# A state-space scan with a three-way maxout FFN: the first block in another order, and weight decoding in portions

## The chip, the cores and the metric

The kernel runs on one core of a Trainium2 chip. The metric is the device time of one execution in microseconds (us). TensorE (PE) has two clock levels, 1.2 and 2.4 GHz; a granted clock of 1.00 in a row is the higher one. PEld is PE's weight load, DVE is VectorE, ACT ScalarE, POOL GpSimd, SP SyncE, which issues DMAs.

## The reference, cut to what matters

```
log_a = log(clip(a, 1e-6, 1))                   # a: (4 batches, 8 heads, 768 steps)
for each chunk:
    cum = cumsum(log_a[chunk])
    L[i,j] = exp(cum[i] - cum[j]) for i >= j, else 0
    y = ((C @ B.T) * L) @ x + (C @ state) * exp(cum)
    state = exp(cum[-1]) * state + sum_j exp(cum[-1] - cum[j]) * B[j] x[j]
X = y as (3072 tokens, 256)
h = max(X @ w1, X @ w2, X @ w3)                 # w: 256 x 768
out = h @ w_out                                 # w_out: 768 x 256
```

x is (4, 8, 768, 32), B and C are (4, 8, 768, 16), all float32. The four weights are float64 in DRAM.

## The kernel before, in words

The 768 steps are cut into NC = 6 blocks of 128 steps; a block holds 4 batches x 8 heads. For a block, B and C are transposed on PE (trB, trC) and copied by ACT to BT and, once for even and once for odd heads, to CT. `scan_scores` makes the products of B and C for two batches in four PSUM banks, and DVE multiplies them into L (L406), which holds the decays exp(cum_i - cum_j). `scan_out` multiplies by x (and, from block 1 on, adds the carried state, L419) and copies y to yT. `scan_state` carries the state on.

The FFN of a block has six up groups, `up(c, f)`, and two down groups, `down(c, u)`. An up group makes three products of yT with w1, w2 and w3, each in one of three PSUM banks of the tag "ffn": ACT copies the first to m (L449), DVE takes the maximum with the second and with the third (L451). A product is four matmul instructions in the trace. A down group multiplies h with w_out, ACT copies the result to ob, and SP stores it.

The order of each engine's work is the order in which the program issues it (a manual schedule). Between the groups of block c, the pieces of the scan of block c + 1 are issued by hand, at group number k.

Decays of block 0 come from `spread_first` (PE spreads cum over the partitions, four banks for two batches; there are five banks of the tag "att"). For batches 0 and 1, POOL fills `below` and DVE adds (L293), then ACT takes exp (L295). For batches 2 and 3, PE adds a mask by a product with the identity (L265) and ACT takes exp with ncum as bias, one head at a time (L301). From block 1 on, cum is stored in DRAM (`cums`), `decay_load` spreads it to all partitions in four DMAs of 512 KB, and a `decay_part` is one POOL select for a batch (L323) and four exps on ACT for half of its heads (L327). `last_load` brings E in eight small DMAs.

A weight is fetched in 12 jobs of 512 KB (nine of w1 to w3, three of w_out) by SP into `rb`. `decode` turns a job to float32: Abs on ACT (L162), a clip (L163) and a shift (L166) on DVE, a scaled copy on ACT (L170), an add on POOL (L171), and the sign step on DVE (L172), which waits for the add. Jobs 0 to 2 serve the first two up groups, 3 to 5 the next two, 6 to 8 the last two, 9 to 11 the down groups. Three jobs are decoded ahead of the FFN, the others after each group of block 0.

SP's queue before: a, B, C, six small loads of the rest of a (a_sb, L110), two jobs, x, one job, cums, three jobs, B and C of block 1, one job, L, x and E of block 1, and then the jobs that are left.

Of the kernel before, what the change touches and what calls it, by code (L numbers as in the profile page):

```python
# [18 lines left out]
def kernel(  # L19
# [24 lines left out]
    P = 128  # L44
# [21 lines left out]
    wraw = ctx.enter_context(tc.tile_pool(name="wraw", bufs=7))  # L66
    wtmp = ctx.enter_context(tc.tile_pool(name="wtmp", bufs=2))
# [39 lines left out]
    a_sb = const.tile([R, 2, P], FP32, name="a_sb")  # L107
    for c in range(NC):
        w, k = divmod(c, NC // 2)
        nc.sync.dma_start(  # L110
            out=a_sb[k * BH:(k + 1) * BH, w], in_=a_rows[:, c * P:(c + 1) * P])


# [33 lines left out]
    def decode():  # L147

        if not fetched:
            return  # L150
# [4 lines left out]
        def temp(name):  # L155
            return wtmp.tile(shape, U32, tag=name, name=name)

        u = temp("w_u")
        nc.scalar.activation(u.bitcast(FP32), hi.bitcast(FP32), AF.Abs)  # L162
        nc.vector.tensor_scalar(  # L163
            out=u.bitcast(FP32), in0=u.bitcast(FP32), scalar1=SMALL, scalar2=LARGE,
            op0=ALU.max, op1=ALU.min)
        nc.vector.tensor_scalar(  # L166
            out=u, in0=u, scalar1=3, scalar2=None, op0=ALU.logical_shift_left)

        r = temp("w_r")
        nc.scalar.activation(r.bitcast(FP32), lo, AF.Copy, bias=2.0, scale=2.0 ** -51)  # L170
        nc.gpsimd.tensor_tensor(out=r, in0=u, in1=r, op=ALU.add)  # L171
        nc.vector.scalar_tensor_tensor(  # L172
            out=dst.bitcast(U32), in0=hi.rearrange("p (k f) -> p k f", k=2), scalar=0x80000000,
            in1=r.rearrange("p (k f) -> p k f", k=2), op0=ALU.bitwise_and, op1=ALU.bitwise_or)

    fetch()
    fetch()
    load(0, "x")
# [22 lines left out]
    mask = const.tile([P, HALF, P], FP32, name="mask")  # L201
    nc.gpsimd.memset(mask, 0.0)
    nc.gpsimd.affine_select(
        out=mask, in_=mask, pattern=[[0, HALF], [1, P]], compare_op=ALU.is_ge, fill=MASKED,
# [5 lines left out]
    def running(rows, src, name):  # L210

        nc.vector.tensor_scalar(
            out=src, in0=src, scalar1=1e-6, scalar2=1.0, op0=ALU.max, op1=ALU.min)
        lg = const.tile(list(src.shape), FP32, name=name + "_lg")
        nc.scalar.activation(lg, src, AF.Ln)
        for w in range(src.shape[1]):
            nc.vector.tensor_tensor_scan(
                out=src[:, w], data0=keep[0:rows], data1=lg[:, w], initial=0.0,
                op0=ALU.mult, op1=ALU.add)
        return src  # L220
# [23 lines left out]
    cum0 = running(P, a0.unsqueeze(1), "first")  # L244
    t = by_token(BH, cum0, "ncum0", -1.0)
    ncum[0] = t[:, 0]
# [13 lines left out]
    def spread_first(b0, masked):  # L260
        for i in range(2):
            for g in range(2):
                spread[b0 + i, g] = bank = att_bank([P, HALF, P], "spread")
                if masked:
                    nc.tensor.matmul(  # L265
                        out=bank.rearrange("p k i -> p (k i)"), lhsT=ident,
                        rhs=mask.rearrange("p k i -> p (k i)"), start=True, stop=False,
                        skip_group_check=True)
        for k in range(HALF):
            for i in range(2):  # L270
                for g in range(2):
                    rows = slice((2 * i + g) * BH, (2 * i + g + 1) * BH)
                    n = (b0 + i) * NH + g * HALF + k
                    nc.tensor.matmul(
                        out=spread[b0 + i, g][:, k],
                        lhsT=pick[rows, n:n + 1].to_broadcast([BH, P]), rhs=cum0[rows, 0],
                        start=(k == 0 and not masked), stop=True,
                        tile_position=((2 * i + g) * BH, 0),
                        skip_group_check=True)

    def below(b):

        t = att.tile([P, NH, P], FP32, tag="below", name="below")
        nc.gpsimd.affine_select(
            out=t, in_=ncum[0][:, b * NH:(b + 1) * NH].unsqueeze(2).to_broadcast([P, NH, P]),
            pattern=[[0, NH], [1, P]], compare_op=ALU.is_ge, fill=MASKED, base=0,
            channel_multiplier=-1)
        return t

    def first_by_sum(b, t):  # L290
        for g in range(2):
            part = L0[:, b, g * HALF:(g + 1) * HALF]
            nc.vector.tensor_tensor(  # L293
                out=part, in0=spread[b, g], in1=t[:, g * HALF:(g + 1) * HALF], op=ALU.add)
            nc.scalar.activation(part, part, AF.Exp)  # L295

    def first_by_bias(b):
        for g in range(2):
            for k in range(HALF):
                h = g * HALF + k  # L300
                nc.scalar.activation(  # L301
                    L0[:, b, h], spread[b, g][:, k], AF.Exp,
                    bias=ncum[0][:, b * NH + h:b * NH + h + 1], scale=1.0)
# [34 lines left out]
    def scan_in(c, bank):  # L338
        st = blocks[c]
        if c < NC - 1:  # L340
            st["Bd"] = Bd = att.tile([P, BH, N], FP32, tag="Bd", name="Bd")
            nc.gpsimd.tensor_tensor(
                out=Bd, in0=st["B"], in1=from_j[c].unsqueeze(2).to_broadcast([P, BH, N]),
                op=ALU.mult)
        tr = {}
        for name in ("B", "C"):
            tr[name] = bank([HN, NB, P], "tr" + name)
            for b in range(NB):
                nc.tensor.transpose(  # L349
                    out=tr[name][:, b],  # L350
                    in_=st[name][:, b * NH:(b + 1) * NH].rearrange("s h n -> s (h n)"),
                    identity=ident)
        st["BT"] = BT = att.tile([HN, NB, P], FP32, tag="BT", name="BT")
        nc.scalar.copy(out=BT, in_=tr["B"])  # L354

        st["CT"] = CT = att.tile([HN, NB, 2, P], FP32, tag="CT", name="CT")
        for g in range(2):
            nc.scalar.mul(CT[:, :, g], tr["C"], parity[:, g:g + 1])
        if c > 0:
# [3 lines left out]
            nc.vector.tensor_tensor(out=Cd, in0=tr["C"], in1=E, op=ALU.mult)  # L363

    def scan_state(c):
        if c == NC - 1:
            return
# [24 lines left out]
    def scan_scores(c, b0):  # L392
        st = blocks[c]
        L = Ls[c]
        banks = [att_bank([P, 2, 2, P], "s") for _ in range(NP)]
        for i in range(2):
            b = b0 + i
            for r in range(NP):
# [4 lines left out]
                    start=(i == 0), stop=True, tile_position=(r * PN, 0), skip_group_check=True)  # L403
        for r in range(NP):
            M = L[:, b0:b0 + 2, 2 * r:2 * r + 2]
            nc.vector.tensor_tensor(out=M, in0=banks[r], in1=M, op=ALU.mult)  # L406

    def scan_out(c):
# [3 lines left out]
        ys = [att_bank([P, NB, P], "y") for _ in range(KD)]  # L412
# [22 lines left out]
    hT = {}  # L435

    def up(c, f):
# [3 lines left out]
        for i in range(3):  # L441
# [27 lines left out]
    spread_first(0, False)  # L469
    from_j[0] = by_token(BH, fj0, "from_j0", 1.0)[:, 0]  # L470
    sums = [below(b) for b in range(2)]
    for b in range(2):
        first_by_sum(b, sums[b])
    scan_in(0, ffn_bank)
    spread_first(2, True)
    cum = running(R, a_sb, "all")
    nc.sync.dma_start(
        out=cums.rearrange("c k s -> (c k) s").rearrange("(w r) s -> r w s", w=2), in_=cum)
    scan_scores(0, 0)
    for b in range(2, NB):  # L480
        first_by_bias(b)
    scan_scores(0, 2)
    fj = from_last(R, cum, "fj")
    ncums = by_token(R, cum, "ncums", -1.0)
    from_js = by_token(R, fj, "from_js", 1.0)
    for c in range(1, NC):
        ncum[c], from_j[c] = ncums[:, c], from_js[:, c]
    for _ in range(3):
        fetch()
    load(1, "B")  # L490
    load(1, "C")
    scan_out(0)
    for _ in range(3):
        decode()
    scan_state(0)
    fetch()
    decay_load(1)
    load(1, "x")
    last_load(1)

    pieces = [(up, f) for f in range(NF)] + [(down, u) for u in range(NB // 2)]
    parts = decay_parts(1)
    for c in range(NC):
        n = c + 1
        for k, (g, i) in enumerate(pieces):
            g(c, i)
            for _ in range(2 - k % 2):
                decode()  # L510
                if weight_jobs:
                    fetch()
            if n < NC:
                if k == 1:
                    scan_in(n, att_bank)
                if k == 3:
                    scan_scores(n, 0)
                if k == 4:
                    scan_state(n)
                if k == 5:  # L520
                    scan_scores(n, 2)
                if k == 6:
                    scan_out(n)
            if n + 1 < NC:
                if k == 4:
                    decay_load(n + 1)
                    load(n + 1, "B")
                    load(n + 1, "C")
                    load(n + 1, "x")
                    last_load(n + 1)  # L530
                    parts += decay_parts(n + 1)
            if k > 0 or c > 0:
                for _ in range(2):
                    if parts:
                        decay_part(*parts.pop(0))
# [30 lines left out]
```

## Time and profile before

| what | value |
|---|---|
| median of 3 runs (range) | 347.91 us (347.3 to 348.58) |
| profiled execution, its own time | 347.55 us |
| its span, first to last instruction | 345.7 us |
| granted PE clock, mean | 0.951 |
| busy share: PE, DVE, ACT, POOL | 92%, 32%, 34%, 15% |

The page gives busy time by engine; the share is a mean over stages. Chains and waits say what ended last in a stage; windows give busy time, granted clock and traffic in a stretch. The execution's own time is 1.85 us more than the span, which the instructions do not cover.

### The profile page before, as it was taken

How to read it: one execution, taken by the hardware profiler on the slowest of the kernel's cores; microseconds unless marked ns; L12 is line 12 of the kernel's file. 1: busy time of each engine (PE TensorE's matmuls, PEld its weight loads, DVE VectorE, ACT ScalarE, POOL GpSimd, SP SyncE). 2: the span in 40 equal slices, each digit the busy share in tenths (PEclk: the TensorE clock that was granted, in tenths of full speed). 3: DMA queues.
4: the chain of work that ended last, by engine and by line, in shares of the span. 5: the costliest groups of instructions: out<-in, count | busy, mean ns of one | idle time of the engine just before them, and what ended most of it. 6: DMA issues, size and time to landing. Idle time of an engine off the chain costs nothing.

```text
span 345.7 us, 4497 instructions
## 1 busy us (share of the span) xinstructions
PE 316.5 (92%) x1742; PEld 180.7 (52%) x1742; DVE 110.8 (32%) x182; ACT 117.1 (34%) x293; POOL 51.8 (15%) x58
## 2 busy tenths in 40 slices
PE   4895978595699999999999999999999999999995
PEld 3464333242486444684444874445854447744474
DVE  3162554573600334401342303354012443022310
ACT  3625445461537400544314272206443010111001
POOL 6002233235520002400006000005000000000000
PEclk9956998879589999999999999999999999999999
DMA  7999889800003960007910019900000000100001
GB/s 74 199 274 255 163 317 279 112 2 0 1 32 101 236 88 2 1 32 254 139 34 1 32 58 247 117 5 2 32 31 0 0 0 2 41 22 0 0 0 61
DMA packets 87333, 28.06 MB, mean 81 GB/s; under 512 B 75537, under 2 KB 81681, under 8 KB 87313
## 3 DMA queue, kind: packets, MB, share of 16 engines
q1 hardware_dynamic: 87216, 27.76, 35.6%
q8 instruction: 13, 0.21, 0.3%
q14 instruction: 8, 0.06, 0.1%
q10 hardware_dynamic: 96, 0.03, 0.0%
HBM read 24.54 MB, written 3.24 MB: 80 GB/s over the span
## 4 chain that ended last, share of the span: by engine, by line
PE 79%; ACT 5%; POOL 5%; DVE 5%; DMA 2%; issue 2%; SPq 0%; POOLq 0%; DVEq 0%; ACTq 0%
PE up L444 48%; PE o L459 19%; PE s L400 4%; PE y L427 4%; POOL w_r L171 3%; ACT L L327 3%; DMA raw_C<-in_C_dram 2%; PE y L419 1%; POOL L L323 1%; PE spread L265 1%; DVE w_u L166 1%; PE trC L349 1%; DVE w_u L163 1%; ACT L L301 1%; DVE w L172 1%
## 5 line engine op out<-in xcount | busy, mean ns | idle before, releaser
L444 PE MATMUL up<-yT,w 128*128 128x512 f32 x432 | 196.4, 610 | 11.8 <-DVE w L172 7.3
L444 PEld LDWEIGHTS up<-yT,w 128*128 128x128 f32 x432 | 82.7, 195 | 112.9 <-issue 92.4
L459 PE MATMUL o<-wo,h 128*128 128x256 f32 x288 | 68.8, 397 | 7.0 <-ACT m L449 5.5
L451 DVE TENSOR_TENSOR m<-m,up 128x512 f32<-128x512 f32 x36 | 24.7, 687 | 146.6 <-PE up L444 77.8
L459 PEld LDWEIGHTS o<-wo,h 128*128 128x128 f32 x288 | 56.1, 198 | 18.7 <-ACT m L449 5.9
L327 ACT ACTIVATE L<-L,ncums 128x128 f32<-128x128 f32 x160 | 48.9, 391 | 43.6 <-POOL L L323 43.6
L449 ACT COPY m<-up 128x512 f32<-128x512 f32 x36 | 20.9, 580 | 87.2 <-PE up L444 87.2
L451 DVE TENSOR_TENSOR h<-m,up 128x512 f32<-128x512 f32 x36 | 24.8, 688 | 27.8 <-PE up L444 27.0
L406 DVE TENSOR_TENSOR L<-s,L 128x512 f32<-128x512 f32 x48 | 29.8, 682 | 9.9 <-PE s L400 9.9
L463 ACT COPY ob<-o 128x512 f32<-128x512 f32 x12 | 7.0, 586 | 51.6 <-PE o L459 40.2
L171 POOL TENSOR_TENSOR w_r<-w_u,w_r 128x512 uint32<-128x512 uint32 x12 | 15.2, 1265 | 60.4 <-DVE w_u L166 55.0
L323 POOL TENSOR_SCALAR_AFFINE_SELECT L<-L 128x1024 f32<-128x1024 f32 x20 | 22.2, 1138 | 0.0
L400 PE MATMUL s<-CT,BT 32*128 32x256 f32 x192 | 18.7, 439 | 1.5 <-ACT L L301 1.5
L400 PEld LDWEIGHTS s<-CT,BT 32*128 32x128 f32 x192 | 11.7, 201 | 11.4 <-issue 7.6
L385 POOL TENSOR_TENSOR old<-S,E 128x256 f32<-128x256 f32 x4 | 2.5, 622 | 76.3 <-issue 76.3
L427 PE MATMUL y<-L,raw_x 128*32 128x128 f32 x384 | 13.4, 299 | 0.0
L172 DVE SCALAR_TENSOR_TENSOR w<-rb,w_r 128x512 uint32<-128x512 uint32 x9 | 8.8, 977 | 13.2 <-POOL w_r L171 13.2
L432 ACT COPY yT<-y 128x512 f32<-128x512 f32 x12 | 6.4, 589 | 18.5 <-PE y L427 18.5
L427 PEld LDWEIGHTS y<-L,raw_x 128*32 128x32 f32 x384 | 11.4, 120 | 1.3 <-issue 0.9
L388 POOL TENSOR_TENSOR S<-S,old 128x256 f32<-128x256 f32 x4 | 2.9, 726 | 47.0 <-DVE S L380 47.0
L162 ACT ACTIVATE w_u<-rb 128x512 f32<-128x512 f32 x12 | 8.1, 672 | 1.4 <-POOL w_r L171 1.4
L354 ACT COPY BT<-trB 128x512 f32<-128x512 f32 x6 | 3.5, 583 | 14.4 <-PE trB L349 14.4
(61 smaller groups left out, 110.2 us busy)
## 6 DMA issues: line engine op xcount, KB each, us to landing
L<-cums SPq DMA_DIRECT2D x20, 512.0 KB, 6.5
rb<-in_moe_w_dram SPq DMA_DIRECT2D x9, 512.0 KB, 5.0
raw_x<-in_x_dram SPq DMA_DIRECT2D x6, 512.0 KB, 7.8
out_dram<-ob SPq DMA_DIRECT2D x12, 256.0 KB, 2.2
raw_B<-in_B_dram SPq DMA_DIRECT2D x6, 256.0 KB, 9.1
raw_C<-in_C_dram SPq DMA_DIRECT2D x6, 256.0 KB, 11.0
rb<-in_moe_w_out_dram SPq DMA_DIRECT2D x3, 512.0 KB, 5.6
E<-cums SPq DMA_DIRECT2D x40, 32.0 KB, 2.3
```

The costliest lines, as they stand in the source:

```text
L162: nc.scalar.activation(u.bitcast(FP32), hi.bitcast(FP32), AF.Abs)
L171: nc.gpsimd.tensor_tensor(out=r, in0=u, in1=r, op=ALU.add)
L172: nc.vector.scalar_tensor_tensor(out=dst.bitcast(U32), in0=hi.rearrange("p (k f) -> p k f", k=2), scalar=0x80000000, in1=r.rearrange("p (k ...
L323: nc.gpsimd.affine_select(out=L[:, b], in_=L[:, b], pattern=[[0, NH], [1, P]], compare_op=ALU.is_ge, fill=MASKED, base=0, channel_multipli ...
L327: nc.scalar.activation(L[:, b, h], L[:, b, h], AF.Exp, bias=ncum[c][:, b * NH + h:b * NH + h + 1], scale=1.0)
L400: nc.tensor.matmul(out=banks[r][:, i].rearrange("j g i -> j (g i)"), lhsT=st["BT"][rows, b], rhs=st["CT"][rows, b].rearrange("p g i -> p ( ...
L406: nc.vector.tensor_tensor(out=M, in0=banks[r], in1=M, op=ALU.mult)
L427: nc.tensor.matmul(out=ys[t][q * D:(q + 1) * D, b], lhsT=st["x"][:, b * NH + h], rhs=M[:, b, h], start=(c == 0 and b == 0), stop=True, til ...
L444: nc.tensor.matmul(out=p, lhsT=w_sb[i][:, k, f * P:(f + 1) * P], rhs=yT[c][:, k], start=(k == 0), stop=(k == KD - 1))
L449: nc.scalar.copy(out=m, in_=p)
L451: nc.vector.tensor_tensor(out=m if i == 1 else hT[c][:, f], in0=m, in1=p, op=ALU.max)
L459: nc.tensor.matmul(out=o[:, i], lhsT=hT[c][:, f, b * P:(b + 1) * P], rhs=wo_sb[:, f], start=(f == 0), stop=(f == NF - 1), skip_group_check ...
```

## The change

The first block is done in another order. The six loads of a_sb go from SP's queue to ACT's, behind the first logarithm. Batch 0 is summed on DVE head by head with the mask as an operand (`scalar_tensor_tensor`); for batches 1 to 3, POOL writes the masked ncum straight into L and DVE adds the spread banks. The mask products on PE and the exps with bias are gone; all exps of block 0 are 512 wide. `scan_in` is cut into `scan_b`, `scan_c` and `scan_bd`. Of the two copies of y, one is done by DVE, in all blocks.

A decode is cut in two: `first` (up to POOL's add) and `second` (the sign step). A call of `decode` issues the first part of one job and then the second part of the job before. One call stands between the two halves of block 0's scores, three behind scan_out, and seven, with the eight decay parts of block 1 and four more calls, are put in a list `fillers`; `up` takes one from it behind each of its three products, `down` one in front of each of its two halves. Decay parts of later blocks go through the same list. The transposes of ncum and from_j for later blocks and `scan_state(0)` stand behind the first up group. In block 0 the scan of block 1 is issued later: transposes at k = 3, scores at 4 and 6, scan_state at 5. There are nine buffers for fetched jobs and three for the decode's temporaries. SP's queue behind cums is now: six jobs, L, E, B, C and x of block 1, three jobs.

```
-    wraw = ctx.enter_context(tc.tile_pool(name="wraw", bufs=7))
-    wtmp = ctx.enter_context(tc.tile_pool(name="wtmp", bufs=2))
+    wraw = ctx.enter_context(tc.tile_pool(name="wraw", bufs=9))
+    wtmp = ctx.enter_context(tc.tile_pool(name="wtmp", bufs=3))
...
+    unsigned = []
+    def decode():
+        steps = decode_steps() if fetched else None
+        if steps:
+            steps[0]()
+        if unsigned:
+            unsigned.pop(0)()
+        if steps:
+            unsigned.append(steps[1])
+
     fetch()
     load(0, "x")
+    fetch()
     fetch()
...
+    cum0 = a0.unsqueeze(1)
+    clip(cum0)
+    lg0 = logs(cum0, "lg0")
+    a_sb = const.tile([R, 2, P], FP32, name="a_sb")
+    for c in range(NC):
+        w, k = divmod(c, NC // 2)
+        nc.scalar.dma_start(
+            out=a_sb[k * BH:(k + 1) * BH, w], in_=a_rows[:, c * P:(c + 1) * P])
+    running(P, lg0, cum0)
...
     def below(b):
         nc.gpsimd.affine_select(
+            out=L0[:, b], in_=ncum[0][:, b * NH:(b + 1) * NH].unsqueeze(2).to_broadcast([P, NH, P]),
...
+    def first_sums(b, filled):
+        for g in range(2):
+            part = L0[:, b, g * HALF:(g + 1) * HALF]
+            if filled:
+                nc.vector.tensor_tensor(
+                    out=part, in0=spread[b, g], in1=part, op=ALU.add)
+            else:
+                for k in range(HALF):
+                    n = b * NH + g * HALF + k
+                    nc.vector.scalar_tensor_tensor(
+                        out=part[:, k], in0=spread[b, g][:, k], scalar=ncum[0][:, n:n + 1],
+                        in1=mask, op0=ALU.add, op1=ALU.add)
+    def first_exps(b):
+        for g in range(2):
+            part = L0[:, b, g * HALF:(g + 1) * HALF]
             nc.scalar.activation(part, part, AF.Exp)
...
-        for t in range(KD):
-            nc.scalar.copy(out=yT[c][:, t], in_=ys[t].rearrange("p b i -> p (b i)"))
+        for t, copy in zip(range(KD), (nc.scalar.copy, nc.vector.tensor_copy)):
+            copy(out=yT[c][:, t], in_=ys[t].rearrange("p b i -> p (b i)"))
...
     def up(c, f):
...
+            fill()
     def down(c, u):
         o = ffn_bank([P, 2, DM], "o")
         for i in range(2):
             b = 2 * u + i
+            fill()
...
+    spread_first(0)
     from_j[0] = by_token(BH, fj0, "from_j0", 1.0)[:, 0]
+    for b in range(1, NB):
+        below(b)
+    first_sums(0, False)
+    first_exps(0)
+    scan_b(0, ffn_bank)
+    spread_first(2)
+    first_sums(1, True)
+    first_exps(1)
+    clip(a_sb)
+    first_sums(2, True)
+    scan_c(0, ffn_bank)
+    lg = logs(a_sb, "lg")
+    first_sums(3, True)
+    first_exps(2)
+    first_exps(3)
+    running(R, lg, a_sb)
     nc.sync.dma_start(
+        out=cums.rearrange("c k s -> (c k) s").rearrange("(w r) s -> r w s", w=2), in_=a_sb)
+    scan_bd(0)
+    s01 = scan_scores(0, 0)
+    scan_weights(0, 0, s01)
+    decode()
+    s23 = scan_scores(0, 2)
+    scan_weights(0, 2, s23)
+    fj = from_last(R, a_sb, "fj")
+    for _ in range(6):
         fetch()
+    decay_load(1)
+    last_load(1)
     load(1, "B")
     load(1, "C")
     load(1, "x")
+    while weight_jobs:
+        fetch()
+    scan_out(0, ffn_bank)
+    decode()
+    decode()
+    decode()
...
+    def first_tokens():
+        ncums = by_token(R, a_sb, "ncums", -1.0)
+        from_js = by_token(R, fj, "from_js", 1.0)
+        for c in range(1, NC):
+            ncum[c], from_j[c] = ncums[:, c], from_js[:, c]
+        scan_state(0)
     pieces = [(up, f) for f in range(NF)] + [(down, u) for u in range(NB // 2)]
+    fillers += 7 * [decode] + decays_of(1) + 4 * [decode]
     for c in range(NC):
         n = c + 1
         for k, (g, i) in enumerate(pieces):
             g(c, i)
+            if c == 0 and k == 0:
+                first_tokens()
             if n < NC:
+                late = 2 if c == 0 else 0
+                if k == 1 + late:
+                    scan_b(n, att_bank)
+                    scan_c(n, att_bank)
+                    if n < NC - 1:
+                        scan_bd(n)
+                if k == 3 + late // 2:
+                    scan_weights(n, 0, scan_scores(n, 0))
+                if k == 4 + late // 2 and n < NC - 1:
                     scan_state(n)
+                if k == 5 + late // 2:
+                    scan_weights(n, 2, scan_scores(n, 2))
                 if k == 6:
+                    scan_out(n, att_bank)
+            if n + 1 < NC and k == 4:
+                decay_load(n + 1)
+                last_load(n + 1)
+                load(n + 1, "B")
+                load(n + 1, "C")
+                load(n + 1, "x")
+                fillers += decays_of(n + 1)
```

## Rows read from the trace of the kernel before

**Rows 1.** The page: busy time by engine, share of the span, instructions.
```profile
PE 316.5 (92%) x1742; PEld 180.7 (52%) x1742; DVE 110.8 (32%) x182; ACT 117.1 (34%) x293; POOL 51.8 (15%) x58
```

**Rows 2.** The chain that ended last: start, duration in us, what.
```profile
28.15 0.59 ACT yT L432
...
31.67 0.69 DVE w L172
32.36 0.35 DVE w_u L163
32.73 0.44 DVE w_u L166
...
33.31 1.27 POOL w_r L171
...
34.60 0.69 DVE w L172
...
107.12 10.30 PE up L444 x24
...
155.69 10.30 PE up L444 x24
```

**Rows 3.** Waits, 0 to 105 us: waiter, waited-for, total us, times, longest.
```profile
ACT L L327 <- POOL L L323: 26.1, 5, 7.8
...
PE up L444 <- DVE w L172: 7.3, 3, 3.7
...
PE o L459 <- ACT m L449: 5.5, 1, 5.5
...
PE up L444 <- ACT m L449: 4.5, 2, 4.2
```

**Rows 4.** Windows: busy of PE, PEld, DVE, ACT, POOL; PE clock; DMA; GB/s.
```profile
50.00:52.00 2.00, 0.00 (x0) 0.00 (x0) 0.91 (x1) 0.00 (x0) 2.00 (x2) 1.00 1.06 391
...
54.00:56.00 2.00, 2.00 (x3) 0.37 (x2) 0.00 (x0) 2.00 (x9) 0.00 (x0) 0.51 1.01 414
```

**Rows 5.** Timeline, 0 to 20 us: start, duration of the group, what.
```profile
0.80 0.90 ACTq L83 DMA_DIRECT2D a<-in_a_dram  x2
...
3.52 0.31 ACT L215 ACTIVATE first_lg<-a 128x128 f32<-128x128 f32 x1 [0.52 <-DVE a L212]
...
4.42 4.52 SPq L110 DMA_DIRECT2D a_sb<-in_a_dram  x6
...
6.85 2.47 DVE L293 TENSOR_TENSOR L<-spread,below 128x512 f32<-128x512 f32 x4
...
9.18 4.80 PE L265 MATMUL spread<-mask,ident 128*128 128x512 f32 x8
...
10.36 1.27 ACT L358 ACTIVATE CT<-trC,parity 128x512 f32<-128x512 f32 x2
...
15.09 4.24 ACT L301 ACTIVATE L<-spread,ncum 128x128 f32<-128x128 f32 x16 [3.17 <-PE spread L274]
```

**Rows 6.** Timeline: DVE operations beside POOL's, two places.
```profile
63.18 1.10 POOL L323 TENSOR_SCALAR_AFFINE_SELECT L<-L 128x1024 f32<-128x1024 f32 x1
63.27 1.55 DVE L172 SCALAR_TENSOR_TENSOR w<-rb,w_r 128x512 uint32<-128x512 uint32 x1 [1.47 <-POOL w_r L171]
...
91.67 4.68 POOL L323 TENSOR_SCALAR_AFFINE_SELECT L<-L 128x1024 f32<-128x1024 f32 x4
...
93.23 2.47 DVE L406 TENSOR_TENSOR L<-s,L 128x512 f32<-128x512 f32 x4
```

**Rows 7.** Timeline of ACT: the eight exps of two decay parts.
```profile
72.05 2.45 ACT L327 ACTIVATE L<-L,ncums 128x128 f32<-128x128 f32 x8 [3.70 <-POOL L L323]
```

**Rows 8.** The page: DMA issues, KB each, median us to landing.
```profile
rb<-in_moe_w_dram SPq DMA_DIRECT2D x9, 512.0 KB, 5.0
```

**Rows 9.** Windows of 5 us; the last column is GB/s.
```profile
15.00:20.00 5.00, 3.52 (x22) 2.05 (x17) 0.39 (x1) 4.77 (x18) 0.00 (x0) 0.84 1.21 267
...
25.00:30.00 5.00, 3.83 (x92) 3.41 (x83) 1.54 (x5) 2.33 (x5) 0.00 (x0) 0.64 0.88 123
```

More of the change, by code (lines that the diff above doesn't have):

```diff
@@ L145, in fetch, with decode_steps @@
             fetched.append((dst, rb))
-    def decode():
-        if not fetched:
-            return
+    def decode_steps():
         dst, rb = fetched.pop(0)
@@ L153, in decode, with first, second @@
         lo, hi = (rb.rearrange("p k f w -> p (k f) w")[:, :, j] for j in range(2))
[L155 to L176, printed above, removed]
+        held = {}
+        def first():
+            u = wtmp.tile(shape, U32, tag="w_u", name="w_u")
+            nc.scalar.activation(u.bitcast(FP32), hi.bitcast(FP32), AF.Abs)
+            nc.vector.tensor_scalar(
+                out=u.bitcast(FP32), in0=u.bitcast(FP32), scalar1=SMALL, scalar2=LARGE,
+                op0=ALU.max, op1=ALU.min)
+            nc.vector.tensor_scalar(
+                out=u, in0=u, scalar1=3, scalar2=None, op0=ALU.logical_shift_left)
+            held["r"] = r = wtmp.tile(shape, U32, tag="w_r", name="w_r")
+            nc.scalar.activation(r.bitcast(FP32), lo, AF.Copy, bias=2.0, scale=2.0 ** -51)
+            nc.gpsimd.tensor_tensor(out=r, in0=u, in1=r, op=ALU.add)
+        def second():
+            nc.vector.scalar_tensor_tensor(
+                out=dst.bitcast(U32), in0=hi.rearrange("p (k f) -> p k f", k=2),
+                scalar=0x80000000, in1=held["r"].rearrange("p (k f) -> p k f", k=2),
+                op0=ALU.bitwise_and, op1=ALU.bitwise_or)
+        return first, second
+    unsigned = []
[7 more added lines that the diff above has]
+            unsigned.append(steps[1])
     fetch()
     load(0, "x")
+    fetch()
     fetch()
@@ L207, with clip, logs, running @@
     nc.vector.memset(keep, 1.0)
-    def running(rows, src, name):
+    def clip(src):
         nc.vector.tensor_scalar(
             out=src, in0=src, scalar1=1e-6, scalar2=1.0, op0=ALU.max, op1=ALU.min)
-        lg = const.tile(list(src.shape), FP32, name=name + "_lg")
+    def logs(src, name):
+        lg = const.tile(list(src.shape), FP32, name=name)
         nc.scalar.activation(lg, src, AF.Ln)
-        for w in range(src.shape[1]):
+        return lg
+    def running(rows, lg, out):
+        for w in range(out.shape[1]):
             nc.vector.tensor_tensor_scan(
-                out=src[:, w], data0=keep[0:rows], data1=lg[:, w], initial=0.0,
+                out=out[:, w], data0=keep[0:rows], data1=lg[:, w], initial=0.0,
                 op0=ALU.mult, op1=ALU.add)
-        return src
     def from_last(rows, cum, name):
@@ L258, with spread_first @@
     spread = {}
-    def spread_first(b0, masked):
+    def spread_first(b0):
         for i in range(2):
             for g in range(2):
[L263 to L268, printed above, removed]
+                spread[b0 + i, g] = att_bank([P, HALF, P], "spread")
         for k in range(HALF):
@@ L336, with scan_b, transposes, scan_c @@
     yT = {}
-    def scan_in(c, bank):
+    def scan_b(c, bank):
         st = blocks[c]
[L340 to L352, printed above, removed]
-        st["BT"] = BT = att.tile([HN, NB, P], FP32, tag="BT", name="BT")
-        nc.scalar.copy(out=BT, in_=tr["B"])
+        tr = bank([HN, NB, P], "trB")
+        transposes(tr, st["B"])
+        st["BT"] = BT = att.tile([HN, NB, P], FP32, tag="BT", name="BT")
+        nc.scalar.copy(out=BT, in_=tr)
+    def transposes(out, raw):
+        for b in range(NB):
+            nc.tensor.transpose(
+                out=out[:, b], in_=raw[:, b * NH:(b + 1) * NH].rearrange("s h n -> s (h n)"),
+                identity=ident)
+    def scan_c(c, bank):
+        st = blocks[c]
+        tr = bank([HN, NB, P], "trC")
+        transposes(tr, st["C"])
         st["CT"] = CT = att.tile([HN, NB, 2, P], FP32, tag="CT", name="CT")
         for g in range(2):
-            nc.scalar.mul(CT[:, :, g], tr["C"], parity[:, g:g + 1])
+            nc.scalar.mul(CT[:, :, g], tr, parity[:, g:g + 1])
         if c > 0:
@@ L403, in scan_scores, with scan_weights, scan_out @@
                     start=(i == 0), stop=True, tile_position=(r * PN, 0), skip_group_check=True)
+        return banks
+    def scan_weights(c, b0, banks):
         for r in range(NP):
-            M = L[:, b0:b0 + 2, 2 * r:2 * r + 2]
+            M = Ls[c][:, b0:b0 + 2, 2 * r:2 * r + 2]
             nc.vector.tensor_tensor(out=M, in0=banks[r], in1=M, op=ALU.mult)
-    def scan_out(c):
+    def scan_out(c, bank):
         st = blocks[c]
@@ L411, in scan_out @@
         yT[c] = ffn.tile([P, KD, BLK], FP32, tag="yT", name="yT")
-        ys = [att_bank([P, NB, P], "y") for _ in range(KD)]
+        ys = [bank([P, NB, P], "y") for _ in range(KD)]
         if c > 0:
@@ L466, in down @@
             in_=ob)
-    spread_first(0, False)
+    spread_first(0)
     from_j[0] = by_token(BH, fj0, "from_j0", 1.0)[:, 0]
[L471 to L476, printed above, removed]
-    nc.sync.dma_start(
[L478 to L481, printed above, removed]
@@ L491, with decays_of @@
     load(1, "C")
[L492 to L497, printed above, removed]
-    load(1, "x")
-    last_load(1)
+    load(1, "x")
+    while weight_jobs:
[4 more added lines that the diff above has]
+    decode()
+    def decays_of(c):
+        if c >= NC:
+            return []
+        return [lambda b=b, g=g: decay_part(c, b, g) for b in range(NB) for g in range(2)]
+    def first_tokens():
[4 more added lines that the diff above has]
+        scan_state(0)
```

77 lines of the change are left out of this document (16 added, 61 removed).

## The prediction

> **What bounds the kernel now.** I read the busy line of the page first: PE is busy for 316.5 of 345.7 us [rows 1]. An average over stages hides where the missing time lies, so the chain that ended last came next. From 107.12 us on it holds nothing but PE work, and blocks follow each other at 155.69 - 107.12 = 48.57 us, two up groups in 10.30 us, so 5.15 us for a group and 1.72 us for one of its three products [rows 2]. All the slack is in front of 107.12: block 0's first product comes behind the decode of w1 at 31.67 + 0.69 = 32.4, and block 0 then needs 74.7 us for what takes a later block 48.57. That is 26 us of stalls and slow clock, behind a prologue of 32 us. The waits up to 105 us name the stalls: PE waits 7.3 us for decoded weights (L172) and 5.5 + 4.5 us for the copy m (L449), and ACT stands 26.1 us at exps that wait for POOL's selects [rows 3]. The m copies are late because they stand behind those exps in ACT's queue, and the selects are late because they stand behind the decode's adds in POOL's. The two windows show what a stall costs on top: after the idle 50 to 52 us PE works at a granted 0.51, its level of 1.2 GHz, although it is busy throughout [rows 4].
>
> So the change can move one number, the time at which block 1 starts: 107.12. Behind it PE has the same products to do, one block after another. Time after = 347.55 (the profiled run, 0.36 below the median of 347.91) minus (107.12 minus the new start).
>
> **Prologue.** Taken out: the eight mask products (9.18 to 13.98) and 16 ACT exps with PSUM input (4.24 us), which stood between B and C's transposes and the scores [rows 5]. Put in: DVE sums for all four batches.
>
> First a small loss. The six a_sb loads now stand on ACT's queue behind the first logarithm (ends 3.83). Two such issues on ACT took 0.90 us, so six take 2.7; SP's six took 4.52, which is the other bound [rows 5]. fj0 then ends at about 6.95, and its transpose and copy stand on PE and DVE in front of the B transposes and the sums: DVE starts the sums at 7.5, not 6.85.
>
> DVE, in order: batch 0 by eight 128-wide sums. The trace has none; a quarter of the 0.62 of a 512-wide sum (2.47 for four) is 0.15, and the whole is 0.62. I take 0.25, nearer the lower end because only the fixed part repeats; 2.0 us, bounds 1.2 to 5. Batch 1: 1.24, to 10.75. The second spread needs the first's banks, so PE does it until 11.6; batches 2 and 3 are summed by 14.1. ACT meanwhile: exps of batch 0 until 10.1, BT 10.7, exps of batch 1 11.9, the two CT muls (1.27) [rows 5] until 14.0, log of the rest 14.4, exps of 2 and 3 until 16.8. The two scans on DVE end at 15.2, so cums leaves at about 15.3, as before.
>
> Scores for batches 0 and 1 run at 14.0 to 15.2, their four products with L on DVE until 17.7, the first decode's clip and shift 0.8 until 18.5, the second four until 21.05. The y products of batches 0 and 1 run meanwhile, so y ends at 21.5, and the two yT copies, now on ACT and DVE side by side, at 22.2. Before it was 28.15 + 0.59 = 28.74 [rows 2]: 6.5 us earlier.
>
> **First products.** Abs of the second decode (an ACT copy of this width takes 0.59), clip 0.35, shift 0.44 and the sign step of the first 0.69 follow: the first product starts at 24.3, 8.1 us earlier than 32.4 [rows 2].
>
> **Decode pace.** This is the dearest unknown. Before, DVE waited for POOL in each decode: sign step to sign step is 34.60 - 31.67 = 2.93 us [rows 2]. Now the sign step of decode k-1 follows the shift of decode k, so that wait has work in it. But the steps do not all run side by side. The sign step, which reads and writes SBUF only, takes 1.55 us instead of 0.69 when POOL's select started 0.09 us earlier: it waits until the select ends at 64.28 and then runs. DVE operations with an input in PSUM do not wait: four products with L took 2.47 us beside four selects [rows 6]. So sign (0.62 from start to start, as those four) and POOL's add (1.27) [rows 2] exclude each other in any case: 1.89 us a decode is the lower bound, 2.93 the upper. The clip and shift of the next decode are SBUF-only too; no row shows them beside POOL. I let them wait as the sign step does, the one SBUF-only form that is shown: 0.35 + 0.44 + 0.62 + 1.27 = 2.7 us. The maxima (0.62, PSUM input) fit beside the add.
>
> The Trainium skill (SBUF — State Buffer, Who interferes with whom) speaks against the pipelining as well: it says that an instruction of tensor_scalar kind in a two-port mode holds the port pair that VectorE and GpSimd share, and that the second to come waits for the whole instruction. No row here shows that kind beside POOL; the sign step's 1.55 us is such a wait for a form with two SBUF inputs. By that rule the clips wait and a decode takes the 2.7; without it 1.89.
>
> In DVE's order decodes 1 to 10 (three calls behind scan_out, then the seven portions behind the first seven products) stand in front of the first maximum of the third up group. Decode 1's clip starts at 22.7; decode 10's at 22.7 + 9 x 2.7 = 47.0; clip and shift, sign step and maximum add 0.8 + 0.6 + 0.6. At 49.0 PE gets a bank for the second product of the fourth group. PE is at most three banks ahead, so until then it goes at DVE's pace: 17 us of products and 2 us of scan_state and transposes in 25 us.
>
> **Rest of block 0.** PE has 48.57 less 3.33 groups of 5.15, so 31.4 us, to do. The eight decay portions now stand one behind each product: four exps take 2.45 / 2 = 1.22 us [rows 7], three of them and an m copy 4.2 us a group, under 5.15. Their selects find POOL free from about 50, 1.1 us each; with BT, CT and E's exp (2.4 us) ACT is nearly full until the sixth group, and I count 0.8 us of PE waiting on it. Decode 11 falls into the sixth group; its sign step and the last maximum keep the down products waiting 1.1 us. Scores and scan_out of block 1 now touch (both behind the first down group): 0.3 us. Block 1 starts at 49.0 + 31.4 + 2.2 = 82.6, 24.5 us earlier. For stretches at half clock, as in [rows 4], I take 1.5 us back (a 2 us window at 0.51 loses 1; none to 4). Gain 23.0, time 324.5.
>
> **Transfers.** On SP's queue the last three weight jobs now stand behind 6 jobs, L (2 MB), E, B, C and x of block 1: 7.3 MB from 15.8 on until the tenth job (number 9) has landed, 0.5 MB for each job [rows 8]. At the 267 GB/s of the window from 15 us that is 27 us: landed at 43. With the 123 of the window from 25 us, in which the small pieces of B and C went, counted as a third, the mean is 219 and it lands at 49 [rows 9]. Its Abs is wanted at about 44. ACT's queue stands still there if it is late, and behind it the m copy of the third group. I take 43, so nothing.
>
> **Later blocks.** One yT copy goes from ACT to DVE, exps move into the groups; both engines are idle there for more than half of the time, and PE has three banks, so I cost this at nothing. If that cover failed it would be dear (below).
>
> **Rivals.**
> - Weights late: job 9 lands at 49, job 10 at 51, so decode 10's clip starts at 51.6 instead of 47.0. For: the tie above. Against: the window of 50 to 52 us reaches 391 GB/s [rows 4]. Time 329.
> - Clips do not wait for POOL: 1.89 us a decode would save up to 7.5 us, but job 10 lands at 41 to 45, so some 5 are left. Time 319.5.
> - The prologue is not earlier: the a_sb issues on ACT take SP's 4.5 us or more and the narrow sums 5 us; the scores wait for both. The decode part of the gain stays. Time 331.
> - Slower: the exps inside the groups get onto PE's path in the later blocks. If each of the eight portions held the m copy, and with it PE, for its 1.22 us, that is 9.8 us a block and 39 us in four blocks: 363. It outweighs the gain from 5.8 us a block on. For: in block 0 PE did wait 10 us for m [rows 3]. Against: there the selects were late, which in later blocks nothing delays.
> - The change does not do it: decode still sets PE's pace at 2.93 and the later portions stall as much as now; within 0.5% only with all of it.
>
> **How the numbers follow.** Forecast 0.50 (its own range 321 to 328, from 1.89 to 2.93 a decode where transfers allow and 0 to 4 for the clock), weights late 0.20, clips free 0.15, prologue not earlier 0.08, slower 0.04, no effect 0.03. The range takes in the first four cases in all but their tails: 316 to 333. A measurement of this kernel can tell about 0.5% (1.7 us) from no change. Faster 0.94, same 0.02, slower 0.04.
>
> **What would show it.** Right: yT of block 0 done at 21 to 24, first product at 23 to 26, POOL's adds 2.6 to 2.9 us apart until 47 to 50, from the fourth group on PE nearly without gaps, block 1 at 80 to 86, later blocks at 48.6. Wrong: adds 2 us apart (clips free); a wait of ACT for the landing of a weight job (weights late); yT after 26; blocks of more than 49 us, with PE waiting for m.

## The result

The changed kernel takes 333.98 us (median of 4 runs, 333.1 to 334.09), the kernel before, run beside it, 347.61: a ratio of 0.9609, 95% interval 0.9564 to 0.9655. Faster, as forecast, but by 13.6 us and not by 23, and 1 us above the upper end of the range. The profiled execution took 334.03 us, its span is 332.3.

The page's busy line, against [rows 1]:

```profile
PE 306.4 (92%) x1734; PEld 176.3 (53%) x1734; DVE 119.6 (36%) x198; ACT 111.7 (34%) x275; POOL 54.6 (16%) x59
```

The chain that ended last, the answer to [rows 2] (start, duration, what):

```profile
6.93 7.56 DMA raw_x<-in_x_dram
14.51 0.32 ACTq L263
...
14.88 0.41 ACT fj L238
...
15.33 0.32 PE from_j_tp L246
...
15.78 0.33 DVE L L311
...
33.67 0.69 DVE w L166
34.35 1.43 DVE w_u L154
...
36.15 0.68 DVE w L166
36.84 1.42 DVE w_u L154
...
41.11 0.68 DVE w L166
41.79 0.60 DVE m L479
...
43.59 0.68 DVE w L166
...
44.92 3.38 PE up L472 x4
...
48.93 6.35 DMA rb<-in_moe_w_out_dram
...
57.67 1.30 DVE w_u L154
...
93.73 10.30 PE up L472 x24
...
142.30 10.30 PE up L472 x24
```

The timeline at the places of [rows 5] and [rows 6]:

```profile
3.68 11.15 ACTq L263 DMA_DIRECT2D a_sb<-in_a_dram  x6
...
15.78 2.15 DVE L311 SCALAR_TENSOR_TENSOR L<-spread,ncum,mask 128x128 f32<-128x128 f32 x8
...
31.91 0.69 DVE L455 COPY yT<-y 128x512 f32<-128x512 f32 x1 [0.99 <-PE y L450]
...
33.90 1.60 POOL L163 TENSOR_TENSOR w_r<-w_u,w_r 128x512 uint32<-128x512 uint32 x1 [3.98 <-DVE w_u L157]
34.27 1.51 DVE L154 TENSOR_SCALAR w_u<-w_u 128x512 f32<-128x512 f32 x1
34.50 6.90 PE L472 MATMUL up<-yT,w 128*128 128x512 f32 x12 [2.67 <-ACT w_r L162]
...
44.92 11.95 PE L472 MATMUL up<-yT,w 128*128 128x512 f32 x24 [1.51 <-DVE h L479]
```

Read from the top. ACT stands at the six a_sb issues from 3.68 to 14.83 us; only then does fj0's exp run, then its transpose on PE, its copy on DVE and the sums. yT is done at 31.91 + 0.69 = 32.6, 3.9 us later than before, and the first product starts at 34.5, 2 us later. Block 1 starts at 93.73 instead of 107.12, and the next one at 142.30: 48.57 us a block, as before. So the whole gain, and more, was made between the first product and block 1, 59 us instead of 75, and the prologue gave part of it back.

| | forecast | measured |
|---|---|---|
| fj0's exp ends | 6.95 | 15.3 |
| yT of block 0 done | 22.2 | 32.6 |
| first product | 24.3 | 34.5 |
| clip of decode 10 starts | 47.0 | 57.7 |
| second product of group 4 | 49.0 | 60.7 |
| block 1 | 84.1 with the clock's 1.5 | 93.7 |
| a later block | 48.57 | 48.57 |

One wait and one pause in the part behind yT: ACT's wait by line (last column: idle before, and for what), and two windows of PE (columns as in [rows 4]):

```profile
L153 ACT ACTIVATE w_u<-rb 128x512 f32<-128x512 f32 x10 | 6.8, 680 | 4.1 <-DMA rb<-in_moe_w_out_dram 4.1
```

```profile
44.00:48.00 4.00, 3.08 (x4) 1.42 (x5) 3.58 (x8) 0.00 (x0) 2.96 (x2) 0.57 0.91 85
48.00:52.00 4.00, 4.00 (x11) 1.72 (x10) 2.45 (x5) 2.89 (x5) 1.43 (x1) 1.00 1.17 149
```

ACT waits 4.1 us for job 9 of the weights. Behind PE's pause near 44 us the next product runs at a granted 0.57: its four instructions take 3.38 us, 1.72 at full clock.

### The profile page after: what moved, and what is told of

The parts are those of the page before. It is cut to its first block, busy times and chain, and to the rows that moved or that the text cites. A ratio compares the mean times of both kernels' runs of the same rounds, so it can differ in the third digit from the quotient of the medians.

```text
span 332.3 us, 4455 instructions
## 1 busy us (share of the span) xinstructions
PE 306.4 (92%) x1734; PEld 176.3 (53%) x1734; DVE 119.6 (36%) x198; ACT 111.7 (34%) x275; POOL 54.6 (16%) x59
## 4 chain that ended last, share of the span: by engine, by line
PE 80%; ACT 5%; DVE 5%; DMA 4%; issue 2%; SPq 2%; POOL 1%; ACTq 0%; POOLq 0%; DVEq 0%
PE up L472 48%; PE o L489 19%; PE s L420 5%; PE y L450 4%; ACT L L342 3%; DMA raw_x<-in_x_dram 2%; DVE w_u L154 2%; DMA rb<-in_moe_w_out_dram 2%; PE y L442 2%; DVE w L166 1%; PE trC L363 1%; PE spread L289 1%; ACT w_u L153 1%; SPq L101 1%; SPq L137 1%
## 5 line engine op out<-in xcount | busy, mean ns | idle before, releaser
L472 PE MATMUL up<-yT,w 128*128 128x512 f32 x432 | 193.2, 603 | 6.0 <-ACT w_r L162 2.7
L489 PE MATMUL o<-wo,h 128*128 128x256 f32 x288 | 65.4, 384 | 0.1
L489 PEld LDWEIGHTS o<-wo,h 128*128 128x128 f32 x288 | 53.8, 190 | 10.4 <-issue 2.8
L163 POOL TENSOR_TENSOR w_r<-w_u,w_r 128x512 uint32<-128x512 uint32 x12 | 18.5, 1540 | 37.8 <-DVE w_u L157 35.3
L338 POOL TENSOR_SCALAR_AFFINE_SELECT L<-L 128x1024 f32<-128x1024 f32 x20 | 21.2, 1092 | 0.0
L420 PE MATMUL s<-CT,BT 32*128 32x256 f32 x192 | 17.6, 446 | 1.4 <-ACT CT L374 1.4
L455 DVE COPY yT<-y 128x512 f32<-128x512 f32 x6 | 4.2, 692 | 25.5 <-PE y L450 25.5
L450 PE MATMUL y<-L,raw_x 128*32 128x128 f32 x384 | 12.4, 285 | 0.0
L154 DVE TENSOR_SCALAR w_u<-w_u 128x512 f32<-128x512 f32 x12 | 10.6, 885 | 4.8 <-ACT w_u L153 4.7
L450 PEld LDWEIGHTS y<-L,raw_x 128*32 128x32 f32 x384 | 10.7, 115 | 1.6 <-issue 1.5
L455 ACT COPY yT<-y 128x512 f32<-128x512 f32 x6 | 3.5, 585 | 17.0 <-PE y L450 17.0
```

Source lines behind the costliest of these rows:

```text
L154: nc.vector.tensor_scalar(out=u.bitcast(FP32), in0=u.bitcast(FP32), scalar1=SMALL, scalar2=LARGE, op0=ALU.max, op1=ALU.min)
L338: nc.gpsimd.affine_select(out=L[:, b], in_=L[:, b], pattern=[[0, NH], [1, P]], compare_op=ALU.is_ge, fill=MASKED, base=0, channel_multipli ...
L420: nc.tensor.matmul(out=banks[r][:, i].rearrange("j g i -> j (g i)"), lhsT=st["BT"][rows, b], rhs=st["CT"][rows, b].rearrange("p g i -> p ( ...
L450: nc.tensor.matmul(out=ys[t][q * D:(q + 1) * D, b], lhsT=st["x"][:, b * NH + h], rhs=M[:, b, h], start=(c == 0 and b == 0), stop=True, til ...
L472: nc.tensor.matmul(out=p, lhsT=w_sb[i][:, k, f * P:(f + 1) * P], rhs=yT[c][:, k], start=(k == 0), stop=(k == KD - 1))
L489: nc.tensor.matmul(out=o[:, i], lhsT=hT[c][:, f, b * P:(b + 1) * P], rhs=wo_sb[:, f], start=(f == 0), stop=(f == NF - 1), skip_group_check ...
```

## The experiments

Theory A: the six issues on ACT stand because of what SP has queued, and that is the missing 8 to 10 us. Theory B: the prologue's new order costs it. Ratios are to the kernel before, run beside it on the same chip; the ratio of the changed kernel is 0.9609, and differences between kernels are taken from the ratios, 0.01 being 3.5 us.

**a_sb back on SP.**

```
     load(0, "C")
+    (the six a_sb loads, on nc.sync)
...
-    (the six a_sb loads, on nc.scalar)
```

> The changed kernel with one thing put back: the six a_sb loads stand on SP's queue behind C again, not on ACT's. Theory A (ACT's six issues stood from 3.68 to 14.83 us because the transfers that SP had queued, x of block 0 above all, had to drain first; fj0, the sums and all that follows were 8 us late): yT of block 0 at 23 to 24 us instead of 32.6, all later work 8 us earlier, 325.5 us. Theory B (the new order of the prologue itself costs the time, the narrow sums and the exps on ACT in front of the scores): less than 2 us, 332 to 334.

325.74 us, ratio 0.9407 (0.9380 to 0.9435). Theory A is right, to 0.3 us. Its timeline and chain:

```profile
4.38 4.58 SPq L109 DMA_DIRECT2D a_sb<-in_a_dram  x6
...
23.31 0.69 DVE L455 COPY yT<-y 128x512 f32<-128x512 f32 x1 [1.35 <-PE y L450]
```

```profile
40.26 6.61 DMA rb<-in_moe_w_out_dram
...
85.33 10.30 PE up L472 x24
```

SP needs 4.58 us for its issues, but no engine's arithmetic stands behind them. yT is done at 24.0 and block 1 starts 8.4 us earlier. This is 1.2 us above my forecast of 324.5: with this one term put right, the rest of the sum holds in total, though not in each term (below).

**fj0's exp in front of the loads.**

```
-    (the six a_sb loads, on nc.scalar)
     running(P, lg0, cum0)
     ncum[0] = by_token(BH, cum0, "ncum0", -1.0)[:, 0]
     fj0 = from_last(BH, cum0, "fj0")
+    (the six a_sb loads, on nc.scalar)
```

> The changed kernel with the exp for fj0 issued on ACT in front of the six a_sb loads, which stay on ACT. Theory A1 (what counts is that fj0's transpose holds PE and its copy holds DVE): sums start at 7 us, but ACT still stands until 14.8, so exps, BT and CT follow from there; scores at 19 instead of 23 us, about 330 us. Theory A2 (any work of ACT behind the loads is as late, so the exps set the time in the same way): within 1 us of the changed kernel, 333 to 334. Theory B: 334.

330.35 us, ratio 0.9531 (0.9501 to 0.9562), as theory A1 has it. Of the 7 us that the loads on ACT cost, about 3 came by fj0 holding PE and DVE (2.7 by the ratios, 3.5 by the start of block 1, 90.26). The others came by ACT's exps and copies behind the issues, which this kernel still holds until 14.6.

**One part alone, on the kernel before.**

> The kernel before with one part of the change alone: its six a_sb loads stand on ACT's queue behind the first logarithm. Theory A: ACT's issues stand until about 15 us here too, BT (9.9 before) and all behind it come 5 to 7 us later, 352 to 354 us. Theory B (ACT had slack there, and the issues cost only their own 2.7 us): 347 to 349.

```
-    (the six a_sb loads, on nc.sync)
...
+    (the six a_sb loads, on nc.scalar, behind running of the first block)
```

352.12 us, ratio 1.0166 (1.0128 to 1.0203). The same part, by itself, makes the kernel before 5.8 us slower, theory A's time, though ACT's issues are over at 12.3 and not at 15. Its timeline:

```profile
3.56 8.75 ACTq L243 DMA_DIRECT2D a_sb<-in_a_dram  x6
```

**Three larger loads on ACT.**

```
-    for c in range(NC):
-        w, k = divmod(c, NC // 2)
-        nc.scalar.dma_start(
-            out=a_sb[k * BH:(k + 1) * BH, w], in_=a_rows[:, c * P:(c + 1) * P])
+    a_parts = a_rows.rearrange("r (w k s) -> k r w s", w=2, k=NC // 2)
+    for k in range(NC // 2):
+        nc.scalar.dma_start(out=a_sb[k * BH:(k + 1) * BH], in_=a_parts[k])
```

> The changed kernel with the a_sb loads still on ACT and behind the first logarithm, but as three DMAs of twice the size instead of six. In the changed kernel ACT's first three issues were out by 5.1 us; the fourth came at 6.0, the fifth at 8.5, the sixth at 14.5. Theory A1 (what stands is each further issue, one at a time, behind the transfers in flight): ACT is free at about 5 us, 325 to 327 us. Theory A2 (what stands is the number of pieces, which is the same): ACT is free at 12 to 15 us, 332 to 334.

324.0 us, ratio 0.9364 (0.9320 to 0.9408). The same bytes in the same pieces, and ACT is free at 5.64:

```profile
3.69 1.95 ACTq L263 DMA_DIRECT2D a_sb<-in_a_dram  x3
...
5.69 0.40 ACT L238 ACTIVATE fj<-a 32x128 f32<-32x128 f32 x1 [1.69 <-DVE ncum L249]
```

So the number of pieces is not what ACT stands for. Whether it is the number of issues or their time, this run can't tell: in the changed kernel too, three issues were out by 5.1 us.

**x of block 0 behind the first three jobs on SP.**

```
     fetch()
-    load(0, "x")
     fetch()
     fetch()
+    load(0, "x")
```

> The changed kernel with one thing moved on SP's queue: x of block 0 stands behind the three first weight jobs, not behind the first. Theory A (ACT's last issues stood for the 4096 pieces of 128 bytes of x): they are out by about 10 us, fj0 comes 4 us earlier, 329 to 330 us. Rival (they stand for any bulk that SP has queued): as the changed kernel, 333 to 334; if x then lands too late for the y products, more.

331.26 us, ratio 0.9563 (0.9519 to 0.9608). ACT stands for 8.38 us instead of 11.15. The result lies between the two: x lengthens the standing, and with the weight jobs alone in front ACT stands too. Timeline:

```profile
3.54 8.38 ACTq L263 DMA_DIRECT2D a_sb<-in_a_dram  x6
```

**Six loads on ACT, but early.**

```
     (table load of ACT)
+    (the six a_sb loads, on nc.scalar)
...
     lg0 = logs(cum0, "lg0")
-    (the six a_sb loads, on nc.scalar)
```

> The changed kernel with the six a_sb loads still on ACT and still six, but issued at once behind the loads of a, in front of the first logarithm, when SP has queued little. Theory S (an issue of ACT stands for the bulk that SP has queued in front of it): six go out at 0.45 us each, the logarithm is at most 1 to 2 us late and fj0 ends at about 6 us, 325 to 327 us. Theory N (only three go out, whatever is queued, and each further one waits for a landing): ACT is free after 8 us at the earliest and the logarithm, which all waits for, is late with it, 329 to 335.

327.73 us, ratio 0.9495 (0.9438 to 0.9551). Neither theory holds by itself. With little but B and C queued the six take half as long, not 2.7 us. Five of them are out by 4.3 us, so theory N's three are no limit; the sixth stands, and goes out from 6.86 to 7.18.

```profile
1.76 5.42 ACTq L98 DMA_DIRECT2D a_sb<-in_a_dram  x6
...
7.29 0.31 ACT L230 ACTIVATE lg<-a 128x128 f32<-128x128 f32 x1 [4.28 <-DMA a_sb<-in_a_dram]
```

So the bulk in flight counts, and with it how many issues are still to come. On what they stand was not found.

**Last weight jobs first.**

```
     last_load(1)
+    while weight_jobs:
+        fetch()
     load(1, "B")
     load(1, "C")
     load(1, "x")
-    while weight_jobs:
-        fetch()
```

> The changed kernel with one thing moved on SP's queue: the last three weight jobs stand in front of B, C and x of block 1. Theory C (ACT's wait of 4.1 us at 51 to 55 for the landing of job 9 is on PE's path): that wait is gone, B and C are still there in time for 64 us, 330 us. Rival: B and C of block 1 land late instead and PE stands at their transposes, 334 to 337; or the wait was covered by DVE's pace, 334.

333.02 us, ratio 0.9607 (0.9569 to 0.9645), the same as the changed kernel by its interval; in the chain block 1 starts at 92.47, 1.3 us earlier. The rival's time is right: little of ACT's 4.1 us had reached PE, which in the changed kernel works without a gap from 44.92 to 56.9 on products whose weights it has. What reached PE is part of a wait for a maximum. Here ACT waits for no weight any more, and of PE's waits (total us, times, longest) that one goes from the first line, the changed kernel's, to the second:

```profile
PE up L472 <- DVE m L479: 1.6, 1, 1.6
PE up L472 <- DVE m L479: 0.5, 1, 0.5
```

```profile
92.47 10.30 PE up L472 x24
```

**Both.** The first experiment's edit and the last.

> a_sb on SP and the last three weight jobs in front of B, C and x of block 1. If the two are independent, 325.7 less the 1.0 to 1.3 us that the second brought alone: 324.5. If with the earlier prologue the weights are later against DVE's pace than before, up to 4 us: 322.

323.90 us, ratio 0.9360 (0.9314 to 0.9406): the 1.6 us by which it lies under 0.9407 is inside the intervals.

**Pipelining undone**, with a_sb on SP.

```
         if steps:
             steps[0]()
-        if unsigned:
-            unsigned.pop(0)()
-        if steps:
-            unsigned.append(steps[1])
+            steps[1]()
```

> a_sb on SP (325.7 us) and the decode not pipelined: the sign step follows the add of its own job at once. Theory D (pipelining saves DVE's wait, 2.48 us a decode against 2.93 and a maximum of 0.62 that no longer lies beside the add, in nine decodes on PE's path): 332 to 335 us. Rival (the shared port leaves the pipelining nothing, or the decode pace is not on PE's path): 326 to 327.

336.21 us, ratio 0.9716 (0.9674 to 0.9758). Theory D holds, though its upper end of 335 falls 1.2 us short. Against 0.9407 the pipelining is worth 10.7 us. POOL's adds:

```profile
27.00 1.27 POOL L168 TENSOR_TENSOR w_r<-w_u,w_r 128x512 uint32<-128x512 uint32 x1 [6.07 <-DVE w_u L162]
29.94 1.27 POOL L168 TENSOR_TENSOR w_r<-w_u,w_r 128x512 uint32<-128x512 uint32 x1 [1.67 <-ACT w_u L158]
...
39.40 1.26 POOL L168 TENSOR_TENSOR w_r<-w_u,w_r 128x512 uint32<-128x512 uint32 x1 [2.29 <-DVE w_u L162]
42.96 1.26 POOL L168 TENSOR_TENSOR w_r<-w_u,w_r 128x512 uint32<-128x512 uint32 x1 [2.29 <-DVE w_u L162]
```

They come 2.95 us apart, and 3.56 where a maximum lies between; in the changed kernel a sign step follows the last in 2.48 with the maximum in it (41.11 to 43.59 in its chain). The rows also show the add at 1.27 where nothing of DVE runs beside it, against 1.60 above.

**The add left out**, a_sb on SP, last jobs first. In the diff is all that it leaves out: POOL's add of the decode.

```
-            nc.gpsimd.tensor_tensor(out=r, in0=u, in1=r, op=ALU.add)
```

> a_sb on SP, last weight jobs first (323.9 us), and POOL's add of the decode left out, so that the weights are not the right ones and POOL does not touch memory beside DVE. Theory F (the clip waits for the add on a shared port): clips take 0.43 us instead of 0.9 to 1.5, a decode 1.5 us plus a maximum 0.6 instead of 2.48, block 1 3 to 5 us earlier, 319 to 321 us. Rival (the long clips are something else, for instance a wait for ACT's result counted into them): clips stay long, 323 to 324.

323.11 us, ratio 0.9353 (0.9299 to 0.9406). The clips are short, as the theory has it; the time is the rival's. Timeline, chain, and a window (columns as in [rows 4]) of this kernel and, below it, of the same kernel with the add:

```profile
25.42 0.42 DVE L159 TENSOR_SCALAR w_u<-w_u 128x512 f32<-128x512 f32 x1
...
30.38 2.58 POOL L337 TENSOR_SCALAR_AFFINE_SELECT L<-L 128x1024 f32<-128x1024 f32 x2 [21.16 <-DMA L<-cums]
...
30.82 1.20 DVE L162 TENSOR_SCALAR w_u<-w_u 128x512 uint32<-128x512 uint32 x1
```

```profile
36.45 18.66 PE up L471 x36
```

```profile
36.00:40.00 4.00, 3.55 (x4) 1.51 (x5) 2.63 (x7) 0.00 (x0) 0.00 (x0) 0.50 0.64 198
36.00:40.00 4.00, 3.31 (x5) 1.45 (x6) 3.34 (x8) 0.25 (x1) 2.72 (x2) 0.69 0.82 248
```

With POOL idle the clip takes 0.42 us; beside a select the shift takes 1.20. But from 36.45 on PE works without a gap: its next 36 instructions take 18.66 us, of which 3.2 are lost to a clock that is at first at 0.50 (24 take 10.30 at full clock). Block 1 starts at 83.78. In the kernel with the add PE already works without a gap from 36.69 on and starts block 1 at 83.56, so there was next to nothing to win: with prologue and weights early, decode no longer holds PE behind the second group.

**Decodes and decay parts by turns**, a_sb in three loads on ACT, with and without the last jobs first.

```
-    fillers += 7 * [decode] + decays_of(1) + 4 * [decode]
+    fillers += 3 * [decode]
+    for n, part in enumerate(decays_of(1)):
+        fillers += [part] + (n < 6) * [decode]
```

> A version meant to beat both: a_sb as three DMAs on ACT, the last weight jobs in front of B, C and x of block 1, and from the second up group on a decay part and a decode by turns instead of seven decodes first. Theory E (what still holds PE in block 0 is seven decodes in a row at 2.48 us against products of 1.72 us): with one decode for two products PE goes at its own pace from the second group on, block 1 starts at 79 to 81 us instead of 83.6, 319 to 321 us. Rival (the selects then compete with adds and clips for the shared port, 3.5 us for two products' 3.44, or the decay parts come before L of block 1 has landed at about 31 us): no gain over 324.

> As the kernel spread_all, but with the last three weight jobs behind B, C and x of block 1 as in the changed kernel. The turns ask for job 9 later, in the sixth product behind the first group (about 46 us): if the landing at about 46 to 47 then costs nothing, the same as spread_all within 0.5 us; if it does, 1 to 3 us more.

324.21 us, ratio 0.9383 (0.9331 to 0.9435), and 325.09, 0.9411 (0.9346 to 0.9475); the second's 1.0 us more is inside the intervals. There is no gain over 0.9364, and theory E fell. It took PE to be held by decodes from the second group on. But in the first kernel without its turns (the last experiment below) PE works without a gap from 39.04 us to the end of the up groups, so there was nothing left to take, and block 1 starts at 82.75, here at 84.46. The turns add two waits of PE (20 to 90 us; total us, times, longest), and the chain shows exps behind selects that stand behind adds on POOL, as before the change:

```profile
PE s L419 <- ACT CT L373: 1.6, 1, 1.6
PE up L471 <- DVE m L478: 0.6, 1, 0.6
```

```profile
46.87 1.56 POOL w_r L163
48.43 1.05 POOL L L337
...
49.51 1.28 ACT L L341 x4
```

**Portions behind the groups**, a_sb on SP.

```
                     out=m if i == 1 else hT[c][:, f], in0=m, in1=p, op=ALU.max)
-            fill()
+        for _ in range(3):
+            fill()
```

> a_sb on SP (325.7 us) and the portions of the list taken three at a time behind each up group instead of one behind each product. Theory G (lying beside the maxima and between the products is worth something): the maxima no longer lie beside the adds, 1.2 us a group in two to three groups, and in all later blocks the m copy stands behind three exp parts, 327 to 331 us. Rival (three banks cover it): 325 to 326.

328.18 us, ratio 0.9505 (0.9447 to 0.9563): 3.4 us for the place between the products. The profile shows 2.6 of it, all in block 0, which ends at 87.94 instead of 85.33; PE there waits 1.76 and 2.11 us for copies m behind the portions. Later blocks keep 48.58, so what was expected of them is wrong.

**What helped, together**: three loads on ACT and the last jobs first.

> The two changes that helped alone, together: a_sb in three DMAs on ACT (324.0 us) and the last three weight jobs in front of B, C and x of block 1 (1.0 to 1.8 us alone). If PE is held by DVE's pace from then on: 322.5 to 323.5; if by its own products at the lower clock, no better than 324.

323.65 us, ratio 0.9362 (0.9323 to 0.9401). No better than the three loads alone; its block 1 starts at 82.75. Three kernels end at 0.936; each beats both kernels of this case.

## Why the prediction was wrong

**The step that failed** is the first of the prologue: "so six take 2.7; SP's six took 4.52, which is the other bound". The six issues took 11.15 us. I priced an issue on ACT by the two at 0.80 us, when hardly anything was in flight, and took the slower of the rows, SP's, for a bound, though they were issued by another queue. fj0 ended 8.3 us late, and the whole table is shifted by that; a_sb on SP gives 7 us of it back (0.9609 to 0.9407). The rival "the prologue is not earlier" had the right place and a chance of 0.08. That its 331 lies 3 us from the result is partly luck: it gave the issues 4.5 us and the narrow sums 5, and they took 11.15 and 2.15. The nearest rows for ACT's price would have been issues with bulk in front of them: in the trace of the kernel before, SP's raw_C issue with B ahead of it took 2.20 us, where B's took 0.42, and a later one, behind three weight jobs and B, 7.39:

```profile
1.72 0.42 SPq L101 DMA_DIRECT2D raw_B<-in_B_dram  x1
...
2.18 2.20 SPq L101 DMA_DIRECT2D raw_C<-in_C_dram  x1
...
18.10 7.39 SPq L101 DMA_DIRECT2D raw_C<-in_C_dram  x1
```

The Trainium skill (DMA: Bandwidth & Descriptors, Issuing engines are not separate DMA queues) says that queues of all engines run on the same DMA engines, and that issuing on several saves only the sequencer's time, which is usually small. The first half fits: ACT stood 11.15 us with x in front on SP's queue and 8.38 with x later. The second does not hold here: the issues held ACT for 11.15 us, and with them back on SP the kernel was 7 us faster.

**From the sums to yT** I was 1.8 us short (24.0 with a_sb on SP, against 22.2). The eight narrow sums were not it, 2.15 for 2.0. In that kernel's timeline DVE could start on the scores 2.1 us after PE did (14.15 to 16.26), where I had 1.2, and y ended 1.3 us behind the last product with L (at 21.96), where I had 0.45.

**Decode pace**: the clips wait for the add, as I had taken them to: 1.51 us beside the add, 0.42 with the add left out. So the rival "clips free" is out. The Trainium skill (SBUF — State Buffer, Who interferes with whom) says that VectorE's tensor_scalar, where it may run in a two-port mode, and a GpSimd instruction exclude each other for a whole instruction; these two rows agree. The size was a little high, 2.7 for 2.48. That the sum to decode 10 still came out (24.8 us behind the first clip, 24.3 forecast) is partly chance: two waits make up for the faster pace, 2.0 us of DVE's behind ACT's wait for job 9, and 1.9 behind an m copy that waited for a product at half clock.

**Weights late** did happen: I had put this at nothing, and ACT waited, as that rival said. With a_sb on SP, job 9 landed at 46.87, 31 us behind the first of the jobs (15.58), between my 27 and 33. (Two slips in my sums change little: by the page's sizes 7.1 MB go up to there, not 7.3, and nine decodes at 0.81 us less give 7.3 us, not 7.5.) It cost 1.3 us and not 4.6, since PE had products to work on meanwhile.

**Rest of block 0**: from the second product of group 4 (60.67) on 33.1 us, forecast 33.6. **Later blocks**: nothing, as forecast. The clock's 1.5 us I cannot check by a run of its own; stretches that began at a granted 0.57 and 0.50 lost 1.7 us (the product at 44.92) and 3.2 (without the add).

**Where the gain came from**: pipelining 10.7 us, the place between products 3.4 us, both taken with a_sb on SP, where the whole gain is 20.6 us (0.9407). They are removals one at a time and need not add up. The new order of the prologue, once a_sb is out of ACT's way, makes yT 4.7 us earlier (24.0 against 28.74). The loads on ACT cost 7.

## What to carry to other kernels

An issue of a DMA on an engine that also computes is an instruction of that engine: put it where nothing waits for that engine's next result, and make few large ones. Price it by issues made while the other queue has bulk in flight, not by those at the start. When a wait is taken away, price the next one in line: here PE's own products stood right behind the waits for weights and decodes. Bringing the weights earlier gave 0.1 us in the changed kernel and 1.6 with a_sb on SP, both inside the intervals, and leaving the add out on top gave 0.2.

## What the runs showed of the hardware

Six issues on ACT's queue stood for 11.15 us with x of block 0 in front, 8.38 with x later, 5.42 when issued early, and three of twice the size for 1.95 at the same place. And leaving POOL's add out made clips 0.42 us and the kernel no faster: PE worked without a gap from 36.45 us on, at first at a granted 0.50, and with the add from 36.69 on.
